# Attention and a feed-forward layer on one core: the second product of the last chunks as Strassen's seven block products

## The chip, the cores and the metric

The program runs on one core of a Trainium2 chip. The metric is the device time of one execution in microseconds (us). The engines are TensorE (PE in the profile; its weight loads are PEld), VectorE (DVE), ScalarE (ACT), GpSimd (POOL) and SyncE (SP, which issues transfers). Each takes its own queue of instructions in order, and an instruction waits at the head of its queue for the semaphores that it names.

## The reference

Sliding-window attention with a linear bias over 8 batches, 8 heads, 576 positions and head width 64; its output, laid out as 4608 tokens of width 512, goes through a feed-forward layer of width 2048. All inputs and outputs are float32.

```python
h = x @ w_in                              # (4608, 512) @ (512, 2048)
g = h * (1.0 / (1.0 + np.exp(-1.702 * h)))
return (g @ w_out).astype(np.float32)     # (4608, 2048) @ (2048, 512)
```

The attention ahead of it is `softmax(q k^T / 8 + slope * -|i - j|)` over the last 128 positions, times `v`.

## The kernel before

Tokens are worked in 18 chunks of 256 (`T`, `NCH`; numbered 0 to 17). The 2048 hidden columns are 16 "f tiles" of 128 (`NF`); two neighbours, 2p and 2p+1, are pair p. A chunk walks over its f tiles in a `Job`. `up` (L947) makes one f tile of the hidden layer with 12 matmuls, each with a moving tile of 256 columns: every float32 operand is split into a high part (a cast to fp32r) and a low part (what the cast left over), and three of the four products of the parts are summed (high by high, high by low, low by high) over four slices of the width 512. ACT then takes the tanh (L961), DVE finishes g (L962), ACT casts it to gh (L497) and POOL takes the rest gl = g - gh (L500). `down` (L969) multiplies this f tile by its rows of w_out: 3 passes (gh by the high part of w, gh by the low part, gl by the high part) for each of the two token halves, 6 matmuls with 512 moving columns, into two banks of PSUM, `acc0` and `acc1`, over all 16 f tiles. `finish` (L982) halves the sums and stores them; for the last chunk DVE and ACT each take half of a row block.

`up` of tile f+1 is put ahead of `down` of tile f in the program, so PE has 12 matmuls to do while ACT, DVE and POOL make g. The attention of later batches is fed in between the f tiles; its last matmuls stand at about 903 us in the trace, and from there on the program holds only the feed-forward layer.

Every operation goes through a planner (`Plan.add`), with a buffer taken from numbered slots of a tag (`buf(pool, shape, dtype, tag, slots)`). Up to a set point (`CUT`) the planner's own order is used; the rest, the last chunks among it, is handed in program order to a scheduler that sets the order in each engine's queue. Which slot an operation's buffer has is fixed before. Tags that matter here: `h` (2 slots of PSUM), `g`, `gh`, `gl` (2 each), `o` (3 slots of 128x512), `xf` (4 slots of 128x1024, the attention's output by chunk), and the PSUM banks `s`, `x`, `t` of the attention. The split weights stay in SBUF as `w1` and `w2`, one tile for each f, with its high and its low part.

## Time and profile before

| | |
|---|---|
| median of 3 runs | 1050.21 us (1050.11 to 1050.41) |
| profiled execution | 1050.36 us, of it the span that the trace covers 1048.6 us |
| PE busy | 1035.2 us, 99% of the span |
| DVE, ACT, POOL busy | 710.6, 620.6, 515.6 us (68%, 59%, 49%) |
| chain that ended last | PE 90%, DVE 6% |

The page of the profile gives the busy time of each engine, the span in 40 slices, the chain of work that ended last, and the costliest groups of instructions. A group's row reads: line, engine, operation, output<-inputs, shapes, count, then busy time and mean ns of one, then the idle time of the engine before them and what ended it. A matmul's recorded length includes its way through the array, so neighbours overlap: the rate is read from how far the starts of a run of matmuls lie apart, which the chain of waits shows.

### The profile page before, as it was taken

The page shows a single profiled execution, that of the slowest core. Times are in us where ns is not written, and L with a number is a line of the kernel's source. Part 1 is how long each engine was busy: PE and PEld are TensorE (multiplying, and loading weights), DVE is VectorE, ACT ScalarE, POOL GpSimd, SP SyncE. Part 2 cuts the span into 40 slices and gives each one's busy share as a digit, 9 for nine tenths or more (in the row PEclk, how much of TensorE's full clock was granted, in tenths as well). Part 3 has the DMA queues.
Part 4 walks back from the last instruction along what each step waited for, and adds up shares of the span by engine and source line. Part 5 has one row for each costly group of instructions (what it writes and reads, how often), then busy time and mean ns, then how long its engine had stood idle before and what let it go on. Part 6 is the DMA issues. An engine that isn't in the chain of part 4 may idle for free.

```text
span 1048.6 us, 21817 instructions
## 1 busy us (share of the span) xinstructions
PE 1035.2 (99%) x6986; PEld 931.0 (89%) x6986; DVE 710.6 (68%) x2418; ACT 620.6 (59%) x1804; POOL 515.6 (49%) x781
## 2 busy tenths in 40 slices
PE   9999999999999999999999999999999999999998
PEld 5777888988988999999999999999999999999997
DVE  8999988898978867444767667666867576412221
ACT  7999877677745665534555556655665566322322
POOL 3344444443423466544655666665766565323232
PEclk9999999999999999999999999999999999999999
DMA  9734233233322222211222223222222120000000
GB/s 342 312 103 132 60 88 100 75 82 104 86 60 68 81 75 69 60 46 29 71 58 60 73 63 89 70 66 59 88 68 85 55 83 17 22 1 22 1 21 21
DMA packets 88033, 80.31 MB, mean 77 GB/s; under 512 B 41776, under 2 KB 78000, under 8 KB 87920
## 3 DMA queue, kind: packets, MB, share of 16 engines
q1 hardware_dynamic: 82736, 69.50, 22.3%
q10 hardware_dynamic: 5184, 9.44, 2.4%
q8 instruction: 55, 0.90, 0.4%
q14 instruction: 58, 0.48, 0.2%
HBM read 69.47 MB, written 9.44 MB: 75 GB/s over the span
## 4 chain that ended last, share of the span: by engine, by line
PE 90%; DVE 6%; issue 2%; ACT 1%; POOL 0%; DVEq 0%; POOLq 0%; ACTq 0%
PE h_ps L953 35%; PE acc L977 35%; PE t_ps L834 5%; PE s_ps L760 5%; PE x_ps L879 5%; PE s_ps L757 1%; PE x_ps L873 1%; DVE pb L779 1%; DVE wc L584 1%; DVE g L962 1%; DVE w_ps L581 1%; PE idle L548 1%; DVE gl L500 1%; DVE xf L924 1%; DVE pl L853 0%
## 5 line engine op out<-in xcount | busy, mean ns | idle before, releaser
L953 PE MATMUL h_ps<-xh,w 128*128 128x256 f32 x2304 | 357.3, 283 | 0.1
L953 PEld LDWEIGHTS h_ps<-xh,w 128*128 128x128 f32 x2304 | 321.2, 188 | 24.3 <-DVE g L962 1.6
L977 PE MATMUL acc<-w,gh 128*128 128x512 f32 x1152 | 320.2, 396 | 0.0
L500 POOL TENSOR_TENSOR gl<-g,gh 128x256 fp32r<-128x256 f32 x225 | 169.1, 752 | 235.6 <-ACT gh L497 178.2
L962 DVE SCALAR_TENSOR_TENSOR g<-g,h_ps 128x256 f32<-128x256 f32 x288 | 120.1, 417 | 186.0 <-ACT g L961 183.7
L961 ACT ACTIVATE g<-h_ps 128x256 f32<-128x256 f32 x288 | 110.2, 383 | 212.9 <-PE h_ps L953 197.4
L977 PEld LDWEIGHTS acc<-w,gh 128*128 128x128 f32 x1152 | 196.0, 188 | 24.4 <-issue 0.2
L953 PE MATMUL h_ps<-xl,w 128*128 128x256 f32 x1152 | 189.4, 279 | 0.0
L977 PE MATMUL acc<-w,gl 128*128 128x512 f32 x576 | 184.3, 397 | 0.0
L953 PEld LDWEIGHTS h_ps<-xl,w 128*128 128x128 f32 x1152 | 160.6, 188 | 4.6
L497 ACT CAST gh<-g 128x256 fp32r<-128x256 f32 x235 | 95.5, 406 | 104.4 <-DVE g L962 97.6
L791 ACT ACTIVATE pb<-pb,mins 128x256 f32<-128x256 f32 (+2 forms) x272 | 132.7, 489 | 39.4 <-DVE mins L779 31.7
L500 POOL TENSOR_TENSOR Q<-rq,Q 64x256 fp32r<-64x256 f32 (+1 forms) x136 | 93.8, 689 | 101.5 <-issue 26.9
L500 POOL TENSOR_TENSOR K<-rk,K 128x384 fp32r<-128x384 f32 (+1 forms) x120 | 108.7, 906 | 61.1 <-PE x_ps L879 19.4
L779 DVE CUSTOM_DVE_ANT_0 pb<-s_ps,bias 128x256 f32<-128x256 f32 (+2 forms) x304 | 111.1, 378 | 10.0 <-PE s_ps L760 4.7
L977 PEld LDWEIGHTS acc<-w,gl 128*128 128x128 f32 x576 | 96.7, 189 | 11.9 <-issue 0.3
L760 PE MATMUL s_ps<-K,Q 128*128 128x256 f32 (+1 forms) x504 | 92.5, 295 | 2.3 <-DVE mins L779 1.3
L834 PE MATMUL t_ps<-ident,pb 128*128 128x128 f32 x516 | 91.4, 273 | 2.7 <-DVE wc L584 2.4
L853 DVE TENSOR_TENSOR pl<-t_ps,ph 128x512 fp32r<-128x512 f32 (+2 forms) x140 | 84.8, 605 | 6.9 <-ACT ph L497 6.3
L497 ACT CAST ph<-t_ps 128x512 fp32r<-128x512 f32 (+2 forms) x134 | 69.6, 519 | 23.9 <-PE t_ps L834 22.7
L760 PEld LDWEIGHTS s_ps<-K,Q 128*128 128x128 f32 x504 | 71.9, 189 | 9.8 <-DVE mins L779 2.0
L813 DVE TENSOR_SCALAR pb<-pb,rec 128x256 f32<-128x256 f32 (+1 forms) x191 | 73.8, 419 | 2.6
(102 smaller groups left out, 1274.3 us busy)
## 6 DMA issues: line engine op xcount, KB each, us to landing
...
```

The source lines that it names most:

```text
L497: (nc.scalar.copy if e == "ACT" else nc.vector.tensor_copy)(dst, src)
L500: (nc.gpsimd if e == "POOL" else nc.vector).tensor_tensor(dst, a, b, ALU.subtract)
L760: nc.tensor.matmul(to, u.Q.t[:, q], ks.t[:, k], start=(z == 0), stop=(z == 1))
L779: add("DVE", lambda b=b, e=e, head=head, ra=ra, rb=rb, cs=cs, on=on: nc.vector.tensor_tensor_reduce(b.p.t[ra:rb, cs:b.end], u.s.t[ra:rb, e ...
L791: nc.scalar.activation(live, live, AF.Exp, bias=u.mins.t[:b.rows, e:e + 1], scale=-1.0, accum_out=u.sums.t[:b.rows, e, 0:1])
L813: (nc.gpsimd if on == "POOL" else nc.vector).tensor_scalar(live, live, rec, None, ALU.mult)
L834: nc.tensor.transpose(u.t.t[:c.n, w:w + b.rows], b.p.t[:b.rows, col:col + c.n], ident[:b.rows, :b.rows])
L853: add("DVE", lambda m=m, a=a, z=z: nc.vector.tensor_tensor(u.pl.t[:m, a:z], u.t.t[:m, a:z], u.ph.t[:m, a:z].bitcast(F32), ALU.subtract), d ...
L953: nc.tensor.matmul(h.t, w.t[:, z, k * P:(k + 1) * P], x[k].t, start=(part == 0 and k == 0), stop=(part == 2 and k == NC - 1))
L961: add("ACT", lambda: nc.scalar.activation(g.t, h.t, AF.Tanh, scale=0.851), act_psum(T), r=[h], w=[g], shift=-NEXT)
L962: add("DVE", lambda: nc.vector.scalar_tensor_tensor(g.t, g.t, 1.0, h.t, ALU.add, ALU.mult), dve_one(T), r=[h], w=[g], shift=-NEXT)
L977: nc.tensor.matmul(acc.t, g.t[:, t * P:(t + 1) * P], w.t[:, z], start=(f == self.f0 and n == 0), stop=(f == self.f1 - 1 and n == 2))
```

## The change

`FAST` names the pairs of f tiles of the last three chunks whose second product is made otherwise: pairs 2 to 6 of chunk 15, and pairs 1 to 6 of chunks 16 and 17; 17 pairs in all. For such a pair the product of a 2x2 block matrix of g (two token halves by two f tiles) and a 2x2 block matrix of w_out (two f tiles by two column halves) is made from seven block products, numbered 1 to 7, in place of eight. Each is again three passes of high and low parts, with 256 moving columns: 21 matmuls in place of 12 with 512 columns.

Three things come beside it. `fold` makes, once for each of pairs 1 to 6, the five sums and differences of blocks of w_out and splits them anew; it is called six times within chunk 15, for pair p+2 at the even tile of pair p, and for pair 1 at f = 10. Its results overwrite parts of `w2` (products 6 and 7) or lie in buffers that the attention no longer needs (`lend`, names `wf_...`). `combine` makes for every fast pair the sums and differences of the blocks of g (`gsum`, `gtrace`) and their parts (`gh`, `gl`, `gd`, `gb`). `gather` adds the products that are held in the banks `s`, `x`, `t` (`m13`, `m45`, `m2`) into the output tile after the last fast pair; products 6 and 7 go straight into `acc0` and `acc1`. Both `wtemp` of `fold` and `gsum`, `gd`, `gb` of `combine` live in the three slots of tag `o`. The bias tables become one tile, so that it can be lent. The store of the last chunk is written by DVE alone.

```diff
+FAST = {NCH - 3: range(2, 7), NCH - 2: range(1, 7), NCH - 1: range(1, 7)}
...
-    bias = [const.tile([P, 2 * P], BF16, name=f"bias{h}") for h in range(H)]
+    bias = const.tile([P, H, 2 * P], BF16, name="bias", tag="bias_0")
...
+    lent = [(att, "ph", 2), (att, "ph", 2), (att, "pl", 2), (att, "pl", 2), (const, "bias", 1), (xp, "xf", XBUFS)]
...
+    def fold(p):
+        f0, f1 = 2 * p, 2 * p + 1
+        half = DM // 2
+        both = buf(xp, [P, 2, DM], F32, "xf", XBUFS, name="wsum")
+        for i, f in enumerate((f0, f1)):
+            on = (nc.vector, "DVE", dve_one(DM)) if i == 0 else (nc.gpsimd, "POOL", pool_two(DM))
+            add(on[1], lambda on=on, i=i, f=f: on[0].tensor_tensor(
+                both.t[:, i], w2[f].t[:, 0].bitcast(F32), w2[f].t[:, 1].bitcast(F32), ALU.add), on[2], r=[w2[f]], w=[(both, i)],
+                port=True, behind=plan.chains["sum"])
+        u, v = (Part(both, i, lambda t, i=i: t[:, i]) for i in range(2))
+        ins = {1: (u, 0, v, 1, ALU.add), 3: (u, 1, v, 1, ALU.subtract), 4: (v, 0, u, 0, ALU.subtract),
...
+        res = {2: Part(w2[f0], "n0", lambda t: t[:, :, :half]), 5: Part(w2[f1], "n1", lambda t: t[:, :, half:])}
...
+        for n, (a, i, b, j, op) in ins.items():
+            at = 0 if temp is None else half
+            if temp is None:
+                held = buf(ffn, [P, DM], F32, "o", 3, name="wtemp")
+            temp = Part(held, at, lambda t, at=at: t[:, at:at + half])
+            if n == 6:
+                m = Part(w2[f0], "n1", lambda t: t[:, :, half:])
+            elif n == 7:
+                m = Part(w2[f1], "n0", lambda t: t[:, :, :half])
+            else:
+                m = lend()
+            (hk, hi), (lk, lo) = side(m, 0), side(m, 1)
+            on, eng, ns = (nc.vector, "DVE", dve_one(half)) if n in (1, 4, 7) else (nc.gpsimd, "POOL", pool_two(half))
+            add(eng, lambda on=on, a=a, i=i, b=b, j=j, op=op, temp=temp: on.tensor_tensor(
+                temp.t, a.t[:, i * half:i * half + half], b.t[:, j * half:j * half + half], op),
+                ns, r=list({id(x): x.key_at() for x in (a, b)}.values()), w=[temp.key_at()], port=True)
+            add("ACT", lambda hi=hi, temp=temp: nc.scalar.copy(hi(), temp.t), act_cast(half), r=[temp.key_at()], w=[hk])
+            on, eng, ns = (nc.vector, "DVE", dve_one(half)) if n in (3, 6) else (nc.gpsimd, "POOL", pool_two(half))
+            add(eng, lambda on=on, hi=hi, lo=lo, temp=temp: on.tensor_tensor(
+                lo(), temp.t, hi().bitcast(F32), ALU.subtract), ns, r=[hk, temp.key_at()], w=[lk], port=True)
+            res[n] = m
...
+        folded[p] = res
...
+            if f // 2 in self.fast:
+                add("ACT", lambda: nc.scalar.activation(g.t, h.t, AF.Tanh, scale=0.851), act_psum(T), r=[h], w=[g], shift=-NEXT)
+                add("DVE", lambda: nc.vector.scalar_tensor_tensor(g.t, g.t, 1.0, h.t, ALU.add, ALU.mult),
+                    dve_one(T), r=[h], w=[g], shift=-NEXT)
+                self.gs[f] = g
+                if f % 2:
+                    self.combine(f // 2)
+                return
...
-                697, r=[g, gh], w=[gl], port=True, shift=-NEXT, ways=less_ways(T), lax=LAX["gl"])
+                697, r=[g, gh], w=[gl], port=True, shift=-NEXT, ways=less_ways(T), lax=LAX["gl"],
+                auto="DVE" if self.fast and f == self.f1 - 1 else "POOL")
...
+        def combine(self, p):
+            a, b = self.gs.pop(2 * p), self.gs.pop(2 * p + 1)
...
+            def cast(x, y, key, to, src, n):
+                add("ACT", lambda: nc.scalar.copy(x.t[:, to], y.t[:, src]), act_cast(n), r=[y], w=[x.key_at(key)], shift=-NEXT)
+            def rest(eng, x, y, h, key, to, src, n):
+                on = nc.vector if eng == "DVE" else nc.gpsimd
+                add(eng, lambda: on.tensor_tensor(x.t[:, to], y.t[:, src], h.t[:, to].bitcast(F32), ALU.subtract),
+                    dve_one(n) if eng == "DVE" else pool_two(n), r=[y, h.key_at(key)], w=[x.key_at(key)], port=True, shift=-NEXT)
...
+            first = [buf(ffn, [P, T], F32R, tag, 2) for tag in ("gh", "gl")]
+            for i, (y, src) in enumerate(((a, lo), (b, hi))):
+                to = slice(i * P, i * P + P)
+                cast(first[0], y, i, to, src, P)
+                rest("POOL", first[1], y, first[0], i, to, src, P)
+            parts(first, (3, 4))
+            both = slice(0, T)
+            sums = buf(ffn, [P, DM], F32, "o", 3, name="gsum")
+            plus("DVE", sums, both, a, both, b, both, ALU.add, T)
+            second = [buf(ffn, [P, T], F32R, tag, 2) for tag in ("gh", "gl")]
+            cast(second[0], sums, 0, both, both, T)
+            rest("DVE", second[1], sums, second[0], 0, both, both, T)
+            parts(second, (5, 2))
+            diffs = slice(T, 3 * P), slice(3 * P, 4 * P)
+            plus("DVE", sums, diffs[0], b, lo, b, hi, ALU.subtract, P)
+            plus("DVE", sums, diffs[1], a, hi, a, lo, ALU.subtract, P)
+            third = buf(ffn, [P, DM], F32R, "o", 3, name="gd")
+            th = [Part(third, z, lambda t, z=z: t[:, z * T:z * T + T]) for z in range(2)]
+            cast(th[0], sums, 0, both, slice(T, DM), T)
+            rest("POOL", th[1], sums, th[0], 0, both, slice(T, DM), T)
+            parts(th, (7, 6))
+            last = buf(ffn, [P, DM], F32R, "o", 3, name="gb")
+            trace = buf(raw, [P, 3 * D], F32, "rv", 2, name="gtrace")
+            corner = [Part(last, z, lambda t, z=z: t[:, z * P:z * P + P]) for z in range(2)]
+            whole = slice(0, P)
+            plus("DVE", trace, whole, a, lo, b, hi, ALU.add, P)
+            cast(corner[0], trace, 0, whole, whole, P)
+            rest("POOL", corner[1], trace, corner[0], 0, whole, whole, P)
+            ms[1] = tuple((x.key_at(), lambda x=x: x.t) for x in corner)
+            self.gs[p] = ms
...
+            if self.apart is None:
+                X = buf(ps, [P, 2, half], F32, "s", 1, name="m13")
+                Y = buf(ps, [P, 2, half], F32, "x", 1, name="m45")
+                Z = buf(ps, [P, 2, half], F32, "t", 2, name="m2")
+                self.apart = {n: (m, i) for n, m, i in ((1, X, 0), (3, X, 1), (4, Y, 0), (5, Y, 1), (2, Z, 0))}
+            ms, ws = self.gs.pop(p), folded[p]
+            for n in (3, 4, 5, 2, 7, 6, 1):
...
+                for k, (g, z) in enumerate(((gh, 0), (gh, 1), (gl, 0))):
+                    wk, w = side(ws[n], z)
+                    def run(n=n, k=k, g=g, w=w, out=out):
+                        nc.tensor.matmul(
+                            out(), g[1](), w(), start=(n in (2, 3, 4) and p == self.fast[0] and k == 0),
+                            stop=(n in (1, 2, 5) and p == self.fast[-1] and k == 2), skip_group_check=True)
+                    add("PE", run, 116, 165, r=[g[0], wk], w=[to if n > 5 else (to, n)], chain="down")
+            if p == self.fast[-1]:
+                self.gather()
...
+                add("DVE", lambda: nc.vector.scalar_tensor_tensor(
+                    o.t[:, t, a:z], src().rearrange("p a n -> p (a n)"), by, o.t[:, t, a:z], ALU.mult, ALU.add), dve_one(z - a),
...
+            halved(0, 0, DM, lambda: X.t, X)
+            halved(1, 0, half, lambda: Y.t[:, :1], Y)
+            halved(1, half, DM, lambda: X.t[:, :1], X)
+            more(0, 0, DM, lambda: Y.t, Y, 0.5)
+            more(0, 0, half, lambda: Y.t[:, 1:], Y, -0.5)
+            more(1, half, DM, lambda: X.t[:, 1:], X, 0.5)
+            more(1, 0, half, lambda: Z.t[:, :1], Z, 0.5)
+            more(1, half, DM, lambda: Z.t[:, :1], Z, -0.5)
...
         def down(self, f):
+            if f // 2 in self.fast:
+                if f % 2:
+                    self.down_fast(f // 2)
+                return
...
+                if self.fast and f == self.f1 - 1:
+                    last.append((n, g, z))
+                else:
+                    add("PE", run, 464, 165, r=[g, (w, z)], w=list(self.acc), chain="down")
+            for t, acc in enumerate(self.acc):
+                for n, g, z in last:
+                    add("PE", lambda t=t, acc=acc, n=n, g=g, z=z: nc.tensor.matmul(
+                        acc.t, g.t[:, t * P:(t + 1) * P], w.t[:, z], start=False, stop=n == 2, skip_group_check=True),
+                        232, 165, r=[g, (w, z)], w=[acc], chain="down")
...
+            if self.fast:
+                o, on = self.out, nc.sync if self.c == NCH - 1 else nc.scalar
                 for t, acc in enumerate(self.acc):
-                    for e, a in (("DVE", 0), ("ACT", half)):
-                        add(e, lambda e=e, t=t, acc=acc, a=a: half_on(e, o.t[:, t, a:a + half], acc.t[:, a:a + half]),
-                            act_psum(half), r=[acc], w=[(o, (t, a))])
+                    add("DVE", lambda t=t, acc=acc: nc.vector.scalar_tensor_tensor(
+                        o.t[:, t], acc.t, 0.5, o.t[:, t], ALU.mult, ALU.add), dve_one(DM), r=[acc], w=[(o, (t,))])
...
+        if j.c in FAST:
+            if j.c == NCH - 3 and f % 2 == 0 and f // 2 + 2 in j.fast:
+                fold(f // 2 + 2)
+            elif j.c == NCH - 3 and f == 10:
+                fold(1)
```

In the rows below a name's number ahead of the last is its slot (`gd_0_14930` lies in slot 0 of its tag). ACT's queue where chunk 14 ends and chunk 15 begins, before (`gh_1_14512` is the cast of f tile 0 of chunk 15):

```order
L961 ACTIVATE g_0_14467<-h_ps_1_14454 128x256
L497 CAST gh_0_14470<-g_0_14467 128x256
L961 ACTIVATE g_1_14509<-h_ps_0_14496 128x256
L497 CAST gh_1_14512<-g_1_14509 128x256
L961 ACTIVATE g_0_14540<-h_ps_1_14527 128x256
L1011 DMA out<-o_0_14522 128x512 x2
L497 CAST gh_0_14543<-g_0_14540 128x256
```

and now (the same cast is `gh_1_14505`):

```order
L658 CAST wf_pl_0_14603<-wtemp_1_14601 128x256
L1045 ACTIVATE g_1_14502<-h_ps_0_14489 128x256
L658 CAST w2_6_0_931<-wtemp_0_14610 128x256
L658 CAST wf_bias_0_14607<-wtemp_0_14610 128x256
L1045 ACTIVATE g_0_14557<-h_ps_1_14544 128x256
L658 CAST w2_7_0_1022<-wtemp_2_14617 128x256
L658 CAST wf_bias_0_14607<-wtemp_1_14601 128x256
L1218 DMA out<-o_0_14515 128x512
L498 CAST gh_1_14505<-g_1_14502 128x256
```

Four casts for `fold`, the tanh of the next f tile and one store stand between the tanh of f tile 0 (`g_1_14502`) and its cast.

POOL's queue late in chunk 15, before (only rests of g and, for the next chunk, of x):

```order
L500 TENSOR_TENSOR gl_0_14859<-g_0_14854,gh_0_14857 128x256
L500 TENSOR_TENSOR gl_1_14885<-g_1_14880,gh_1_14883 128x256
L500 TENSOR_TENSOR xl0_0_14927<-xf_1_12925,xh0_0_14919 128x256
L500 TENSOR_TENSOR xl2_0_14931<-xf_1_12925,xh2_0_14923 128x256
L500 TENSOR_TENSOR gl_0_14911<-g_0_14906,gh_0_14909 128x256
```

and now, from the last rests of pair 4 (`gd_0_14930`, `gb_2_14935`) to those of pair 5, with `fold` of pair 1 between them:

```order
L1070 TENSOR_TENSOR gd_0_14930<-gsum_1_14922,gd_0_14930 128x256
L1070 TENSOR_TENSOR gl_1_15020<-g_0_14951,gh_1_15018 128x128
L1070 TENSOR_TENSOR gl_1_15020<-g_1_15015,gh_1_15018 128x128
L1070 TENSOR_TENSOR gb_2_14935<-gtrace_0_14933,gb_2_14935 128x128
L655 TENSOR_TENSOR wtemp_1_14978<-wsum_2_14975 128x256
L660 TENSOR_TENSOR wf_K2_1_14982<-wtemp_1_14978,wf_K1_0_14980 128x256
L655 TENSOR_TENSOR wtemp_0_14989<-wsum_2_14975 128x256
L660 TENSOR_TENSOR wf_VV_1_14993<-wtemp_0_14989,wf_VV_0_14991 128x256
L660 TENSOR_TENSOR w2_3_0_634<-wtemp_2_14998,w2_3_0_634 128x256
L1070 TENSOR_TENSOR gd_0_15032<-gsum_1_15024,gd_0_15032 128x256
L1070 TENSOR_TENSOR gb_2_15037<-gtrace_1_15035,gb_2_15037 128x128
L1070 TENSOR_TENSOR gl_1_15095<-g_1_15090,gh_1_15093 128x128
```

Five rows for `fold` stand between the rests of two pairs; `wtemp_0_14989` is written in the slot that held `gd_0_14930`.

PE's queue at the same place, before (second product of f tile 11 amid the up product of f tile 13):

```order
L977 MATMUL acc0_0_14547<-w2_11_0_1482,gh_0_14805 128x512
L977 MATMUL acc1_0_14549<-w2_11_0_1482,gh_0_14805 128x512
L977 MATMUL acc0_0_14547<-w2_11_0_1482,gh_0_14805 128x512
L977 MATMUL acc1_0_14549<-w2_11_0_1482,gh_0_14805 128x512
L953 MATMUL h_ps_1_14841<-xh3_0_14486,w1_13_0_1734 128x256
L953 MATMUL h_ps_1_14841<-xh0_0_14480,w1_13_0_1734 128x256
L953 MATMUL h_ps_1_14841<-xh1_0_14482,w1_13_0_1734 128x256
L977 MATMUL acc0_0_14547<-w2_11_0_1482,gl_0_14807 128x512
L977 MATMUL acc1_0_14549<-w2_11_0_1482,gl_0_14807 128x512
L953 MATMUL h_ps_1_14841<-xh2_0_14484,w1_13_0_1734 128x256
```

and now (L1134 is a block product; the last readers of `gd_0_14930`, then what is left until the sums of pair 5, `gh_0_15026`):

```order
L1134 MATMUL acc0_0_14564<-w2_9_0_1265,gd_0_14930 128x256
L1134 MATMUL acc1_0_14566<-w2_8_0_1149,gd_0_14930 128x256
L1029 MATMUL h_ps_1_15077<-xl0_0_14481,w1_13_0_1727 128x256
L1029 MATMUL h_ps_1_15077<-xl1_0_14483,w1_13_0_1727 128x256
L1029 MATMUL h_ps_1_15077<-xl2_0_14485,w1_13_0_1727 128x256
L1029 MATMUL h_ps_1_15077<-xl3_0_14487,w1_13_0_1727 128x256
L1134 MATMUL m45_0_14751<-wf_pb_1_14787,gl_1_15020 128x256
L1134 MATMUL m13_0_14747<-wf_xf_0_14674,gb_2_14935 128x256
L1134 MATMUL m13_0_14747<-wf_Q_0_14781,gh_1_15018 128x256
L1134 MATMUL m13_0_14747<-wf_pb_3_14783,gh_1_15018 128x256
L1134 MATMUL m13_0_14747<-wf_Q_0_14781,gl_1_15020 128x256
L1134 MATMUL m45_0_14751<-w2_11_0_1475,gh_0_15026 128x256 x2
```

Nine matmuls stand between the last reader of `gd_0_14930` and the first reader of `gh_0_15026`. ACT's queue at this place now:

```order
L658 CAST wf_K1_0_14980<-wtemp_1_14978 128x256
L658 CAST wf_K2_0_14985<-wtemp_1_14978 128x256
L658 CAST wf_VV_0_14991<-wtemp_0_14989 128x256
L658 CAST w2_2_0_588<-wtemp_0_14989 128x256
L658 CAST w2_3_0_634<-wtemp_2_14998 128x256
L1066 CAST gh_0_15026<-gsum_1_15024 128x256
L1036 ACTIVATE g_1_15090<-h_ps_1_15077 128x256
```

`gh_0_15026` stands behind the casts of all temporaries of `fold`, two of them made from `wtemp_0_14989`.

## Rows read from the trace of the kernel before

**Rows 1.** The page: busy time by engine; granted clock and POOL in 40 slices.
```profile
PE 1035.2 (99%) x6986; PEld 931.0 (89%) x6986; DVE 710.6 (68%) x2418; ACT 620.6 (59%) x1804; POOL 515.6 (49%) x781
...
POOL 3344444443423466544655666665766565323232
PEclk9999999999999999999999999999999999999999
```
**Rows 2.** Busy time of each engine in four stretches of the end.
```profile
core 0: us, PE busy (x) PEld busy (x) DVE busy (x) ACT busy (x) POOL busy (x), PEclk, DMA share, GB/s
870.00:913.00 43.00, 43.00 (x299) 39.78 (x298) 22.23 (x74) 20.54 (x58) 18.35 (x30) 1.00 0.03 7
913.00:957.00 44.00, 44.00 (x285) 39.90 (x285) 10.40 (x25) 12.48 (x32) 13.74 (x18) 1.00 0.03 13
957.00:1002.00 45.00, 45.00 (x294) 40.92 (x293) 11.81 (x26) 12.98 (x33) 13.30 (x18) 1.00 0.03 12
1002.00:1044.00 42.00, 42.00 (x271) 37.86 (x269) 7.32 (x18) 12.00 (x31) 11.80 (x16) 1.00 0.04 13
```
**Rows 3.** Chain of waits, 912 to 922: start, length, what.
```profile
914.03 1.38 PE h_ps L953 x12
915.42 1.37 PE acc L977 x6
916.79 1.39 PE h_ps L953 x12
```
**Rows 4.** Groups by form, 880 to 1049.
```profile
L500 POOL TENSOR_TENSOR gl<-g,gh 128x256 fp32r<-128x256 f32 x58 | 43.0, 741 | 108.5 <-ACT gh L497 89.6 <-PE acc L977 6.2 <-issue 3.7
...
L962 DVE SCALAR_TENSOR_TENSOR g<-g,h_ps 128x256 f32<-128x256 f32 x57 | 24.0, 421 | 108.9 <-ACT g L961 108.8
L497 ACT CAST gh<-g 128x256 fp32r<-128x256 f32 x58 | 23.6, 408 | 33.2 <-DVE g L962 31.7 <-PE acc L977 1.4
L961 ACT ACTIVATE g<-h_ps 128x256 f32<-128x256 f32 x57 | 21.9, 385 | 75.4 <-PE h_ps L953 74.7 <-POOL xb L900 0.6
...
L500 POOL TENSOR_TENSOR VV<-rv,VV 128x128 fp32r<-128x128 f32 x3 | 1.4, 457 | 0.5 <-ACT VV L497 0.5
...
L497 ACT CAST VV<-rv 128x128 fp32r<-128x128 f32 x3 | 0.9, 300 | 0.3 <-PE x_ps L879 0.3
```
**Rows 5.** Groups by form, whole span: POOL, DVE and ACT on 512 columns.
```profile
L500 POOL TENSOR_TENSOR w<-wc,w 128x512 fp32r<-128x512 f32 x11 | 14.2, 1287 | 12.0 <-ACT g L961 8.2 <-ACT rw L579 2.0 <-ACT w L497 1.6
...
L506 DVE TENSOR_SCALAR o<-acc 128x512 f32<-128x512 f32 x29 | 19.0, 683 | 2.4 <-PE acc L977 2.4
...
L504 ACT ACTIVATE o<-acc 128x512 f32<-128x512 f32 x3 | 1.8, 598 | 0.0
```
**Rows 6.** DVE at L500: shortest, median, longest ns; first and last start.
```profile
L500 DVE TENSOR_TENSOR gl<-g,gh x63: 405/425/1006, 33.0 to 355.5; 128x256 fp32r<-128x256 f32 x63
L500 DVE TENSOR_TENSOR xl<-xf,xh x39: 408/826/1175, 71.8 to 997.8; 128x256 fp32r<-128x256 f32 x39
L500 DVE TENSOR_TENSOR VV<-rv,VV x22: 216/306/628, 177.7 to 352.2; 128x128 fp32r<-128x128 f32 x13, 128x64 fp32r<-128x64 f32 x7, 128x192 fp32r<-128x192 f32 x2
L500 DVE TENSOR_TENSOR w<-wc,w x21: 669/685/1254, 16.0 to 132.8; 128x512 fp32r<-128x512 f32 x21
```
**Rows 7.** Timeline at 951 us, DVE, then POOL: start, length, what.
```profile
951.54 1.84 DVE L500 TENSOR_TENSOR xl<-xf,xh 128x256 fp32r<-128x256 f32 x2
...
951.33 0.89 POOL L500 TENSOR_TENSOR gl<-g,gh 128x256 fp32r<-128x256 f32 x1 [1.82 <-PE h_ps L953]
952.18 1.81 POOL L500 TENSOR_TENSOR xl<-xf,xh 128x256 fp32r<-128x256 f32 x2
```
**Rows 8.** Timeline, one f tile of the last chunk, and a store on ACT's queue.
```profile
1039.45 0.62 PE L953 MATMUL h_ps<-xl,w 128*128 128x256 f32 x4
...
1040.17 0.39 ACT L961 ACTIVATE g<-h_ps 128x256 f32<-128x256 f32 x1 [0.57 <-PE h_ps L953]
1040.59 0.42 DVE L962 SCALAR_TENSOR_TENSOR g<-g,h_ps 128x256 f32<-128x256 f32 x1 [1.43 <-ACT g L961]
...
1041.09 0.41 ACT L497 CAST gh<-g 128x256 fp32r<-128x256 f32 x1 [0.54 <-DVE g L962]
...
1041.59 0.74 POOL L500 TENSOR_TENSOR gl<-g,gh 128x256 fp32r<-128x256 f32 x1 [1.18 <-ACT gh L497]
...
1002.43 0.34 ACTq L1011 DMA_DIRECT2D out<-o  x1
```
**Rows 9.** The end of the chain of waits.
```profile
1040.07 3.90 PE acc L977 x17
1043.97 0.02 issue
1044.00 0.44 DVE o L506
...
1044.45 0.71 ACT o L504 x2
```

More of the change, by code (lines that the diff above doesn't have):

```diff
@@ L590, in decode, with lend @@
         return res
+    lent = [(att, "ph", 2), (att, "ph", 2), (att, "pl", 2), (att, "pl", 2), (const, "bias", 1), (xp, "xf", XBUFS)]
+    for pool, tag, slots, n in (
+            (raw, "rq", 3, 3), (att, "Q", 2, 2), (att, "pb", 5, 5), (raw, "rk", 3, 3), (att, "K1", 2, 2),
+            (att, "K2", 2, 2), (att, "VV", 3, 3)):
+        lent += [(pool, tag, slots)] * n
+    spare = []
+    folded = {}
+    def lend():
+        if not spare:
+            pool, tag, slots = lent.pop(0)
+            if tag in ("bias", "xf"):
+                b = buf(pool, [P, 2, 2, DM // 2], F32R, tag, slots, name=f"wf_{tag}")
+                spare.extend(Part(b, i, lambda t, i=i: t[:, i]) for i in range(2))
+            elif tag in ("ph", "pl"):
+                spare.append(Part(buf(pool, [P, 2, DM // 2], F32R, tag, slots, name=f"wf_{tag}"), 0, lambda t: t))
+            else:
+                pair = []
+                for _ in range(2):
+                    size = 3 * P if tag in ("rk", "K1", "K2", "VV") else 2 * P
+                    pair.append(Part(buf(pool, [P, size], F32R, tag, slots, name=f"wf_{tag}"), 0, lambda t: t[:, :2 * P]))
+                    if len(pair) < 2:
+                        pool, tag, slots = lent.pop(0)
+                spare.append(tuple(pair))
+        return spare.pop(0)
@@ L945, in __init__ @@
             self.gs = {}
+            self.fast = FAST.get(c, ())
+            self.apart = None
         def up(self, f):
@@ L972, in down @@
             gh, gl = self.gs.pop(f)
-            w = w2[f]
+            w, last = w2[f], []
             for n, (g, z) in enumerate(((gh, 0), (gh, 1), (gl, 0))):
```

48 lines of the change are left out of this document (40 added, 8 removed).

## The prediction

> **What bounds the kernel now.** I read the page first, then the busy times of the last 180 us, the chain of waits there, the durations of single operations by form, and last the places where DVE and POOL work side by side. The page says PE: 99% of the span at the full granted clock, 2.4 GHz in the last slices too [rows 1]. In the stretches that the last three chunks fill, PE is busy all the time, while DVE, ACT and POOL have 10 to 14 us of work in 42 to 45 us [rows 2]. So in these chunks only less work on PE can gain, and three engines are two thirds idle. The chain gives PE's true rate: 12 matmuls of 256 columns take 1.38 us and 6 of 512 columns 1.37 us [rows 3], 0.115 and 0.228 us each. An up product has as many weight loads per column as a block product will have, and they already hide at this rate.
>
> **What the change removes.** A pair's second product is now 2 x 1.37 = 2.74 us of PE. The new one is 21 matmuls of 256 columns, 21 x 0.115 = 2.415 us. That is 0.325 us less, for 17 pairs 5.5 us. Nothing else leaves the path, and this is the most that it can give.
>
> **What it adds in chunks 16 and 17.** A fast pair has, on POOL, three rests of 128 columns and one of 256, 3 x 0.457 + 0.741 = 2.1 us; on ACT two tanh, three casts of 128 and two of 256, 2 x 0.385 + 3 x 0.300 (by the casts of the same width) + 2 x 0.408 = 2.5 us [rows 4]; on DVE two g at 0.421, two sums of 256 columns at about 0.41 and three of 128 at about 0.3, 2.6 us [rows 4, 6]. PE needs 2.76 (two up products) + 2.415 = 5.2 us for the pair, so each engine is half idle. Latency: tanh, g, cast and rest follow each other at 0.1, 0.03, 0.08 and 0.09 us [rows 8]. From the end of the odd tile's up product, the sums of g are cast after 0.10 + 0.39 + 0.03 + 0.42 + 0.03 + 0.41 + 0.04 + 0.41 = 1.8 us, and the last rest on POOL is done after some 3.5 us. In the new order PE has the next tile's up product, product 3 and in most pairs a second up product ahead of the others, 1.38 + 0.345 + 1.38 = 3.1 us, and product 1 stands 1.7 us behind that. Nothing waits; I take 0 here. If that cover went, a wait of 0.3 us in each of 11 pairs would cost 3.3 us.
>
> **The end.** Before, the last store could be issued 1045.16 - 1043.97 = 1.19 us after the last matmul [rows 9]. Now products 1 are complete 12 matmuls of 512 columns, 2.74 us, before the end. ACT takes 0.60 us for the first halving; DVE then has one addition of 512 columns and three of 256, and the two final ones of 512: 3 x 0.683 + 3 x 0.421 = 3.31 us [rows 4, 5]. That ends 0.1 + 0.60 + 3.31 - 2.74 = 1.27 us after the last matmul: 0.1 us later than before.
>
> **What it adds in chunk 15.** Here `fold` comes on top. One fold is on POOL one sum of 512 columns and five operations of 256: 1.287 + 5 x 0.741 = 5.0 us; on DVE as many of its own kinds, 0.685 + 5 x 0.41 = 2.7 us; on ACT five casts, 2.0 us [rows 4 to 6]. With `combine` POOL has 7.1 us for a pair where PE has 5.2. The folds begin when the attention ends, so POOL starts with a lead and loses it. Three places decide.
>
> First, f tile 0 of the chunk. Its tanh can end 0.10 + 0.39 us after its up product. ACT then takes, in order, four casts for `fold`, a tanh, a store (0.34) and only then this tile's cast: 4 x 0.408 + 0.385 + 0.34 + 0.408 = 2.77 us, 3.3 us in all [rows 4, 8]. PE has 14 matmuls of 256 columns and 2 of 512 in between, 2.07 us. It waits 1.2 us.
>
> Second, POOL from the last rest of pair 2 to the last of pair 5, where the folds of pairs 5 and 6 and of pair 1 lie: 18 operations of 256 columns, 9 of 128 and 2 of 512, 18 x 0.741 + 9 x 0.457 + 2 x 1.287 = 20.0 us. PE has 163 matmuls of 256 columns in that stretch, 18.7 us. POOL's lead at its start is what pair 2 leaves: its last rest can be done 3.5 us after the up product of f tile 5, and PE wants it after 6.1 us (53 matmuls), so 2.6 us. Alone, POOL would be in time by 1.3 us.
>
> But DVE has 21 operations of 256 columns, 2 of 512 and 9 of 128 with both inputs in SBUF in the same stretch, and such operations get in POOL's way. At 951.5 us two of them and three of POOL's overlap: the two on DVE take 0.92 us each where 0.41 is the least, and POOL's two take 1.81 us where 2 x 0.741 would be 1.48 [rows 4, 6, 7]; a typical one of chunk starts takes 0.826 [rows 6]. So a DVE operation of 256 columns costs POOL 0.9 - 0.741 = 0.17 us. By width, 21 x 0.17 + 2 x 0.34 + 9 x 0.09 = 5.1 us if POOL is always busy. Then POOL is late by 5.1 - 1.3 = 3.8 us.
>
> Third, the slots of `o`. The second half of `wtemp_0_14989` is written by POOL where `gd_0_14930` lay, thus after PE has read that. Then ACT casts it, casts another, and casts the sums of pair 5: 0.741 + 3 x 0.408 + about 0.2 of handovers = 2.2 us, in which PE has 9 matmuls, 1.0 us. PE waits 1.2 us here whatever else happens, and through that wait POOL's other work does not start earlier.
>
> Bounds for the second and third together: 1.2 us (only the slot) from below. From above DVE's own queue, if each of its operations with two SBUF inputs is held up as in rows 7: 21 x 0.92 + 2 x 1.25 (the longest of 512 columns) + 9 x 0.6 (the longest of the narrow ones) + 6 g x 0.421 = 29.7 us against PE's 18.7, 11.0 us late [rows 4, 6, 7]. I take POOL's 3.8 and the slot's 1.2, 5.0 us: POOL is busy nearly all the time in this stretch, which is the case of rows 7, but DVE is not, and meets a free port in part.
>
> The early part of the folds (the sums for pair 2) lies amid the attention of chunk 14, where POOL has 18 us of work in 43 [rows 2]; I cost it at nothing, and its 1.3 us at most if POOL's cover there is gone. The merged bias tables move no work; 0.
>
> **Sum.** -5.5 + 0.1 + 1.2 + 5.0 = +0.8 us against the profiled execution's own 1050.36 us (span 1048.6 and 1.8 around it), 1051.2; that execution lies 0.15 us above the median of the runs, so 1051.0 us as a median.
>
> **The rivals.** A measurement of this kernel tells about 0.2%, 2.1 us, from no change.
>
> (A) My forecast: waits of chunk 15 between 3.3 and 7.5 us eat the gain. 1048.1 to 1052.3 us, likeliest 1051.0. For it stand POOL's sum and the slots. Chance 0.40.
>
> (B) Only the two fixed waits are real, 1.2 + 1.2 us: POOL and DVE meet seldom, as on those copies of rows 6 that took the least time. -5.5 + 0.1 + 2.4 = -3.0, 1047.2 us. For it: three engines have room outside of this chunk, and POOL's sum alone fits. Against it: in chunk 15 both engines work on the same tiles back to back. Chance 0.28.
>
> (C) DVE becomes the bound in pairs 3 to 5, since each of its operations with two SBUF inputs waits for the POOL operation that runs: 11.0 + 1.2 us of waits, +6.8, 1057.0 us at the full price. It decides for slower as soon as waits pass 7.5 us, thus DVE's queue 18.7 + 6.3 = 25.0 us there; between 15.1 us (all at their least: 21 x 0.41 + 2 x 0.685 + 9 x 0.3 + 2.5) and 29.7 that is two thirds of the way, a mean of 0.75 us for 256 columns. Rows 6 and 7 have 0.826 and 0.92, which speaks for it; that DVE also runs while POOL waits for ACT's casts speaks against it. Chance 0.32; I expect 1053 to 1056 us in this case.
>
> The Trainium skill, page "SBUF — State Buffer", section "Who interferes with whom", states a lock where I sum a cadence: a DVE operation with two SBUF inputs and a GpSimd operation exclude each other for the whole instruction. By it each DVE operation would add its own length to POOL's queue, an estimate of 12.6 us in the three pairs where I have 5.1, and the change would end at about +8 us, on the side of (C). The trace agrees in kind, not in size: the pair takes 0.92 us there, not 0.41 + 0.741 = 1.15 [rows 4, 6, 7], so the sum stays with 0.92.
>
> That the change would not shorten PE's work (a matmul of 256 columns costing more than half of one of 512) is excluded by rows 3.
>
> **How the numbers follow.** Faster by over 0.2% is case B, 0.28; within 0.2% case A, 0.40; slower case C, 0.32. The range reaches from the price of B, 1047.3 us, to where C's own range ends with less than a tenth above, 1055.5 us. Within A alone it is 1048.1 to 1052.3.
>
> **What would show it.** In the new profile PE's work must be 5.5 us less, and PE must have idle time in chunk 15 alone: about 1 us ahead of the first down product of f tile 0, waiting for ACT, and most of the rest in pairs 3 to 5, ahead of products 5 and 2 and of the rests of 6 and 7. Chunks 16 and 17 must each be shorter by 6 x 0.325 = 2.0 us and show no wait. DVE's sums of 256 columns in chunk 15 must have a mean between 0.6 and 0.9 us, and near 0.41 would be case B. The forecast is wrong if PE waits in chunks 16 and 17, if the tail grows by more than 0.5 us, or if the attention of chunk 14 gets longer.

## The result, and the profile after

The changed kernel takes 1063.35 us (1062.24 to 1064.47, four runs) where the kernel before took 1050.24 us (1050.11 to 1050.41): a ratio of 1.0125, 95% interval 1.0107 to 1.0142. It is slower by 13 us. Case C of the prediction came, at about twice its full price of 6.8 us. The profiled execution is one of 1062.38 us, its span 1060.6 us.

The page after, busy time by engine and four of its lines of 40 slices; it answers to [rows 1]:

```profile
PE 1036.1 (98%) x7139; PEld 937.4 (88%) x7139; DVE 779.5 (73%) x2557; ACT 644.2 (61%) x1892; POOL 558.6 (53%) x848
...
PE   9999999999999999999999999999999999889998
...
DVE  8999988899978868445758576757766685876464
...
POOL 3353544344423566445656566656766574884342
PEclk9999999999999999999999999999999999999999
```

Apart from the last slice, PE is below 9 only where chunk 14 ends and chunk 15 runs, and there DVE and POOL go up to 8. DVE's busy time grew by 68.9 us over the whole span; the operations that were added come to some 55 us at the lengths that they have alone (17 x 1.8 for the sums of g, 6 x 2.7 for the folds, 3 x 2.8 for the gathering and a last rest).

Busy time in stretches of the last 200 us, from the last 50 us of the attention to the last matmul; it answers to [rows 2]:

```profile
core 0: us, PE busy (x) PEld busy (x) DVE busy (x) ACT busy (x) POOL busy (x), PEclk, DMA share, GB/s
855.00:880.00 25.00, 24.14 (x167) 21.91 (x166) 21.07 (x71) 14.98 (x46) 18.01 (x27) 1.00 0.19 55
...
904.00:920.00 16.00, 12.60 (x77) 10.46 (x75) 12.11 (x21) 6.29 (x18) 13.32 (x16) 1.00 0.00 1
920.00:973.00 53.00, 46.14 (x331) 43.40 (x332) 41.30 (x80) 23.60 (x69) 38.39 (x51) 0.97 0.03 11
973.00:1015.00 42.00, 42.00 (x339) 41.12 (x339) 24.17 (x62) 18.36 (x54) 17.08 (x29) 1.00 0.04 14
1015.00:1056.00 41.00, 41.00 (x325) 39.76 (x324) 20.68 (x53) 17.31 (x52) 15.24 (x27) 1.00 0.04 14
```

Chunks 16 and 17 (the last two rows) show no wait of PE, as forecast; they are 1.6 and 1.9 us shorter than before, where 2.0 us each were forecast. Between 904 and 973 us DVE is busy for 53 of 69 us; in a chunk of before it was 10 of 44.

What PE waited for from 860 us on, but for two waits of 0.5 us or less (line, releaser, sum, times, longest):

```profile
PE m L1134 <- DVE gl L1070: 3.0, 2, 2.6
PE h_ps L1029 <- DVE g L1046: 2.8, 2, 2.4
PE m L1134 <- ACT gh L1066: 2.3, 2, 2.0
PE h_ps L1029 <- DVE g L1037: 1.5, 2, 1.4
PE h_ps L1029 <- DVE xh L498: 0.6, 2, 0.3
```

The releasers are DVE, and ACT's cast of a sum that DVE had just made. POOL, which the forecast held to be the late engine, is not in the list. It does stand in the chain of waits behind it: from 917 to 962 us the chain has 20.0 us of DVE and 7.2 us of POOL, all of POOL's before 933.4 us. DVE's queue ahead of the longest wait (timeline, with POOL's operations at the time; PE's row at its end):

```profile
945.39 0.92 POOL L655 TENSOR_TENSOR wtemp<-wsum 128x256 f32<-128x256 f32 x1
...
945.63 0.95 DVE L655 TENSOR_TENSOR wtemp<-wsum 128x256 f32<-128x256 f32 x1
...
947.18 2.12 DVE L1075 TENSOR_TENSOR gsum<-g 128x128 f32<-128x128 f32 x2
...
947.81 1.34 POOL L634 TENSOR_TENSOR wsum<-w 128x512 f32<-128x512 f32 x1
949.12 0.77 POOL L660 TENSOR_TENSOR w<-wtemp,w 128x256 fp32r<-128x256 f32 x1
949.23 1.21 DVE L634 TENSOR_TENSOR wsum<-w 128x512 f32<-128x512 f32 x1
...
950.36 0.41 DVE L1070 TENSOR_TENSOR gl<-gsum,gh 128x256 fp32r<-128x256 f32 x1
...
950.82 0.51 PE L1134 MATMUL m<-w,gl 128*128 128x256 f32 x2 [2.60 <-DVE gl L1070]
```

Two sums of 128 columns take 0.82 and 1.38 us (one row, 2.12 us), and `wsum` of a later fold stands ahead of the `gl` that PE needs. As soon as POOL is done (949.89 us) DVE's operations take 0.41 us again.

The same groups of DVE over 855 to 973 us, mean ns of one after the comma; they answer to [rows 5, 6]:

```profile
L655 DVE TENSOR_TENSOR wtemp<-wsum 128x256 f32<-128x256 f32 x18 | 13.4, 768 | 6.3 <-PE acc L1134 3.7 <-POOL wsum L634 2.0 <-POOL gd L1070 0.6
L1046 DVE SCALAR_TENSOR_TENSOR g<-g,h_ps 128x256 f32<-128x256 f32 x24 | 9.9, 414 | 6.3 <-ACT g L1045 6.2
L634 DVE TENSOR_TENSOR wsum<-w 128x512 f32<-128x512 f32 x6 | 5.6, 940 | 0.1
...
L1075 DVE TENSOR_TENSOR gsum<-g 128x128 f32<-128x128 f32 x10 | 5.4, 562 | 0.1
```

Where the time went is read from five landmarks in the timelines, all of them PE's: the start of the last matmul of the attention, and the start of the last second-product matmul of chunks 14, 15, 16 and 17. Each is set against the kernel before, so that a column's steps are what each stretch lost. (`no_fold` and `fold_only` are told of below.) The profiled executions of `no_dve_fold`, `after_pin` and `early_fold` lost 3.9 us in their first 24 us, so only distances within these traces are used.

| us against before | attention's end | chunk 14 | chunk 15 | chunk 16 | last matmul |
|---|---|---|---|---|---|
| before, at | 902.6 | 913.6 | 957.2 | 1001.5 | 1043.8 |
| changed | +1.7 | +3.6 | +15.6 | +14.0 | +12.1 |
| no_fold | -0.1 | -0.1 | -1.1 | -2.8 | -4.8 |
| fold_only | +1.5 | +3.4 | +10.6 | +9.9 | +9.9 |

### The profile page after: what moved, and what is told of

It reads as the page before. It is cut to its first block, busy times and chain, and to the rows that moved or that the text cites. A ratio compares the mean times of both kernels' runs of the same rounds, so it can differ in the third digit from the quotient of the medians.

```text
span 1060.6 us, 22523 instructions
## 1 busy us (share of the span) xinstructions
PE 1036.1 (98%) x7139; PEld 937.4 (88%) x7139; DVE 779.5 (73%) x2557; ACT 644.2 (61%) x1892; POOL 558.6 (53%) x848
## 4 chain that ended last, share of the span: by engine, by line
PE 82%; DVE 11%; issue 3%; ACT 2%; POOL 1%; DVEq 0%; ACTq 0%; POOLq 0%
PE h_ps L1029 32%; PE acc L1177 28%; PE s_ps L834 5%; PE t_ps L908 5%; PE x_ps L953 5%; PE m L1134 2%; PE x_ps L947 1%; PE s_ps L831 1%; PE acc L1134 1%; DVE g L1046 1%; DVE pb L853 1%; DVE xf L998 1%; DVE wc L585 1%; DVE pl L927 1%; DVE w_ps L582 1%
## 5 line engine op out<-in xcount | busy, mean ns | idle before, releaser
L1177 PE MATMUL acc<-w,gh 128*128 128x512 f32 x1004 | 279.9, 397 | 0.3 <-DVE o L507 0.3
L501 POOL TENSOR_TENSOR gl<-g,gh 128x256 fp32r<-128x256 f32 x188 | 141.5, 753 | 147.6 <-ACT gh L498 104.4
L1177 PEld LDWEIGHTS acc<-w,gh 128*128 128x128 f32 x1004 | 170.9, 189 | 22.1 <-issue 0.6
L1045 ACT ACTIVATE g<-h_ps 128x256 f32<-128x256 f32 x254 | 97.0, 382 | 150.9 <-PE h_ps L1029 134.6
L1046 DVE SCALAR_TENSOR_TENSOR g<-g,h_ps 128x256 f32<-128x256 f32 x254 | 105.6, 416 | 82.5 <-ACT g L1045 80.3
L1177 PE MATMUL acc<-w,gl 128*128 128x512 f32 x502 | 161.0, 398 | 0.0
L498 ACT CAST gh<-g 128x256 fp32r<-128x256 f32 x201 | 81.4, 405 | 86.4 <-DVE g L1046 80.3
L1177 PEld LDWEIGHTS acc<-w,gl 128*128 128x128 f32 x502 | 84.3, 189 | 10.2 <-issue 0.3
L834 PEld LDWEIGHTS s_ps<-K,Q 128*128 128x128 f32 x504 | 71.8, 189 | 10.6 <-DVE mins L853 2.8
```

Of the source, the lines that this page charges most:

```text
L498: (nc.scalar.copy if e == "ACT" else nc.vector.tensor_copy)(dst, src)
L501: (nc.gpsimd if e == "POOL" else nc.vector).tensor_tensor(dst, a, b, ALU.subtract)
L834: nc.tensor.matmul(to, u.Q.t[:, q], ks.t[:, k], start=(z == 0), stop=(z == 1))
L1045: add("ACT", lambda: nc.scalar.activation(g.t, h.t, AF.Tanh, scale=0.851), act_psum(T), r=[h], w=[g], shift=-NEXT)
L1046: add("DVE", lambda: nc.vector.scalar_tensor_tensor(g.t, g.t, 1.0, h.t, ALU.add, ALU.mult), dve_one(T), r=[h], w=[g], shift=-NEXT)
L1177: nc.tensor.matmul(acc.t, g.t[:, t * P:(t + 1) * P], w.t[:, z], start=(f == self.f0 and n == 0), stop=(f == self.f1 - 1 and n == 2), skip_ ...
```

## The experiments

Theory D: the meeting of DVE and POOL on operations with both inputs in SBUF makes each of DVE's take twice its time; DVE's queue, with g and the sums of g in it behind fold's operations, is what PE waits for. Rivals: P, POOL's queue (the forecast); S, the mere number of fold's instructions ahead of g; K, `combine` rather than `fold`. Times are medians against a kernel before of 1050.1 to 1050.2 us.

**no_fold**: the products without the folds.

```diff
-                fold(f // 2 + 2)
+            for p in range(1, 7):
+                folded[p] = {n: Part(w2[2 * p + n % 2], ...) for n in range(1, 8)}
```

> The sums of w_out's blocks are left out (each block product reads an unsummed block of w_out), the products and the sums of g stay. Theory D (DVE's queue: fold's operations with two SBUF inputs wait there for POOL's, and g and the sums of g stand behind them): nothing of fold is left, so no wait is left; 1050.2 - 5.5 + 0.1 = 1044.8 us, between 1044.3 and 1046. Rival K (the sums of g, made by combine, are what PE waits for): waits in chunk 15 stay, above 1049 us.

Measured 1045.73 us, ratio 0.9956 (0.9938 to 0.9973), and not one wait of PE after 855 us. K falls. It also measures the first term of the sum: 4.8 us by the landmarks, 0.28 us a pair, where 5.5 was forecast. The last matmul starts 4.8 us before the span's end in the kernel before and 4.7 us before it here and in the changed kernel, so the end costs nothing.

**fold_only**: the folds without the products.

```diff
-            self.fast = FAST.get(c, ())
+            self.fast = ()
```

> The folds stay where they are, every second product is made as before (from w_out's tiles, parts of which the folds overwrite), the end of the last chunk as before. Theory D: the losses ahead of chunk 15 and at its start (about 6 us) stay whole, and a good part of the 8 us of pairs 2 to 6; 1056 to 1064 us. Rival K: fold alone costs nothing, 1050 to 1052 us.

Measured 1059.98 us, ratio 1.0091 (1.0061 to 1.0122). The loss up to chunk 14's end is nearly the changed kernel's (3.4 of 3.6 us), and 7.2 us more come in chunk 15. Folds alone cost 9.9 us, and 16.9 us together with `combine` (changed less no_fold in the table). One of PE's waits after 855 us is for POOL here:

```profile
PE acc L1177 <- POOL gl L501: 2.0, 2, 1.1
```

From 917 to 968 us the chain of waits has 19.0 us of POOL and 2.8 us of DVE. So without `combine` it is POOL's queue that is late, as rival P has it; with `combine` on DVE it is mostly DVE's.

**no_pool_fold** and **no_dve_fold**: one engine's half of the folds left out.

```diff
+            if eng == "POOL":   # in the other kernel "DVE"
+                temp = ...      # a block of wsum that the other engine made; no instruction
+            else:
                 add(eng, ...)
```

> POOL's part of fold is left out (its sums and rests; what needed them reads DVE's), DVE's and ACT's part stays: DVE issues the same instructions. Theory D: DVE's sums of 256 columns go from a mean of 0.77 to between 0.41 and 0.5 us, PE's waits after 855 us from about 14 to below 3 us, 1045 to 1048 us. Rival S (the number of fold's instructions in DVE's queue, contention or not): waits of 8 us or more stay, above 1053 us. Theory P (as forecast: POOL's queue is what is late): 1045 to 1048 us too, but what is left of waits is for ACT or POOL.

> DVE's part of fold is left out, POOL's (5.0 us for each pair) and ACT's stay. Theory D: DVE holds only what combine and the g need, PE waits below 3 us, 1045 to 1048 us. Rival S the same. Theory P: POOL's own queue of 20.0 us against PE's 18.7 with a lead of 2.6 us fits only just, and combine's sums of g still meet it; waits for POOL's rests of 1 to 4 us in pairs 3 to 5, 1046 to 1049 us.

Measured 1047.07 us (ratio 0.9965, 0.9951 to 0.9980) and 1049.62 us (0.9983, 0.9965 to 1.0002). What PE waits for in `no_pool_fold` after 855 us, and DVE's sums there (L669 is L655 of the changed kernel):

```profile
PE h_ps L1046 <- DVE g L1063: 1.1, 1, 1.1
```

```profile
L669 DVE TENSOR_TENSOR wtemp<-wsum 128x256 f32<-128x256 f32 x18 | 8.4, 484 | 0.8 <-PE acc L1151 0.4 <-POOL gd L1087 0.2 <-PE m L1151 0.2
```

The same 18 sums now take 0.48 us, not 0.77, and 1.1 us of waits is left. S falls here: the number of instructions did not change. Over no_fold, DVE's half costs 1.3 us by itself, POOL's 3.9 us, and both together 17.6 us: 12 us come only when both halves run. This counts everything that one half does to the other, the results that DVE awaits from POOL too. Of these the changed kernel shows 2.6 us ahead of DVE's `wtemp` (2.0 and 0.6 in the first group of DVE above). Longer operations weigh more: from 855 to 973 us DVE's 67 operations with both inputs in SBUF take 18.4 us more than at the lengths that they have with no operation of POOL beside them (0.41 us for 256 columns, 0.29 for 128; 0.68 for 512, from the kernel before).

`no_dve_fold` missed D's range by 1.6 us and P's by 0.6, and chunk 15 is 3.3 us longer there than in no_fold. POOL's queue is not what is late: PE's waits after 855 us, 1.5 us in all, end with DVE or with ACT's cast of a sum, and no POOL operation stands in the chain of waits from 917 to 965 us. DVE's sums of 128 columns stand in it, 0.73 us each in the mean where POOL's half of the folds runs beside them. This is D's mechanism on `combine`'s own operations, which D's number left out.

**all_dve**: the same folds, all on DVE.

```diff
-            on = (nc.vector, "DVE", dve_one(DM)) if i == 0 else (nc.gpsimd, "POOL", pool_two(DM))
+            on = (nc.vector, "DVE", dve_one(DM))
```

and so for the sums and the rests of a fold.

> All of fold's sums and rests are made by DVE, none by POOL; the same work otherwise. Theory D (the price lies in the meeting of the two engines: an operation of DVE with two SBUF inputs takes 0.41 us alone, 0.77 and more beside POOL): a fold is 10 x 0.41 + 2 x 0.685 = 5.5 us on DVE, six are 33 us; with some 20 us of older work and 9 us of combine DVE has 62 us where PE has 55, so it is still the bound, but less than before: 1047 to 1054 us. Rival S (the number of fold's instructions ahead of g in DVE's queue decides): DVE has twice as many of them, waits double, above 1068 us.

Measured 1054.19 us, ratio 1.0039 (1.0024 to 1.0054), the last matmul of the profiled execution 9.1 us earlier than in the changed kernel. DVE has twice the sums, and they are short:

```profile
L655 DVE TENSOR_TENSOR wtemp<-wsum 128x256 f32<-128x256 f32 x30 | 13.2, 484 | 0.9 <-POOL gd L1070 0.6 <-PE acc L1134 0.2
```

The same work on one engine in place of two saves 9 us, which speaks for D most plainly; S, which had over 1068 us for twice the instructions, falls. The median lies 0.2 us over D's range. But 8.5 us over no_fold stay: from 914 to 964 us the chain of waits has 18.4 us of DVE and none of POOL (one wait of PE, 1.0 us, is for a rest of POOL's). So about half of the folds' price goes when the two engines no longer meet over them, and half stays, mostly as DVE's load.

**late_fold**: block products in chunks 16 and 17 alone, the fold of a pair two tiles after its use in chunk 15.

```diff
-FAST = {NCH - 3: range(2, 7), NCH - 2: range(1, 7), NCH - 1: range(1, 7)}
+FAST = {NCH - 2: range(1, 7), NCH - 1: range(1, 7)}
-            if j.c == NCH - 3 and f % 2 == 0 and f // 2 + 2 in j.fast:
+        if j.c == NCH - 3 and f % 2 == 0 and f >= 4:
+            fold(f // 2 - 1)
```

> Only chunks 16 and 17 are made with block products; in chunk 15 the fold of pair p stands two f tiles after the pair's own use, and chunk 15 is otherwise as before. PE's work shrinks by 12 x 0.27 to 0.33 = 3.2 to 3.9 us. Theory D: with no fold while the attention ends and with no combine in chunk 15, the meeting of DVE and POOL costs DVE 6 x (5 x 0.9 + 1) = 33 us in a chunk of 44 us where its older work is 10 us, just below PE; waits of 0 to 4 us: 1046.5 to 1051 us. If each fold costs PE what it does in fold_only (9.9 us for six) whatever its place: 1056 to 1057 us.

Measured 1058.74 us, ratio 1.0079 (1.0062 to 1.0096): above both ranges. The attention ended 1.9 us later than before and chunk 14 2.8 us later, though no fold stands there in the program. The scheduler sends the first sums of folds far ahead of their place, DVE's first `wsum` at 858.1 us (in the changed kernel 857.9), so the place in the program decides little.

**after_pin**: the changed kernel with each sum of a fold held in its queue behind the g of its own f tile (on POOL behind the rest of g).

```diff
+            if op.hold:
+                tc.add_manual_dep(op.made, op.hold.made.name, ...NoSync...)
```

> The changed kernel with its folds at their places, but each sum of a fold (on DVE and on POOL) is held in its queue behind the g, or the rest of g, of the f tile at which the program has it: nothing of a fold can start amid the attention any more. Theory D (DVE and POOL together have more work in chunk 15 than PE): the loss ahead of chunk 15 (1.7 us in the attention, about 4 at its end) goes, but the folds come later and pairs 2 to 6 wait longer, 8 to 14 us; 1056 to 1064 us in all. Theory S (only the order was wrong): the waits go with the order, 1046 to 1050 us.

Measured 1069.82 us, ratio 1.0163 (1.0122 to 1.0203), above both ranges. The attention runs free (chunk 14 takes 55.4 us from the last chunk's end, before 55.4), and chunk 15 takes 64.6 us, before 43.6. Busy time, and PE's largest wait after 855 us:

```profile
905.00:920.00 15.00, 15.00 (x101) 13.78 (x101) 7.76 (x17) 4.41 (x12) 7.06 (x10) 1.00 0.05 20
920.00:970.00 50.00, 36.61 (x234) 33.30 (x233) 40.57 (x69) 22.37 (x66) 45.03 (x54) 0.89 0.02 6
```

```profile
PE m L1138 <- ACT gh L1068: 10.1, 4, 3.7
```

With all folds packed into chunk 15 POOL is busy for 45 of 50 us and DVE for 41: in this order there is no room for them. Holding the sums behind g does not bring the time back, so that only the order was wrong falls as a theory. The chain of waits from 918 to 983 us has 16.9 us of POOL and 8.9 us of DVE, so here POOL's queue is the later one. D's number missed the clock too, which stood at 0.89 of full speed over these 50 us; this cost at most 5.5 us, since PE also waited in part of that time.

**early_fold**: the same folds in chunks 8 to 13, kept in DRAM and loaded where fold stood.

```diff
+            d = scratch[p, n] = buf(dram, [P, 2, half], F32, ...)
+            add("SP", lambda: nc.sync.dma_start(d.t, m.t.bitcast(F32)), ...)
...
+        if 1 <= j.c - EARLY <= 6:
+            if f == 1:
+                sums(j.c - EARLY)
+            elif f in (2, 4, 7, 10, 13):
+                fold_early(j.c - EARLY, {2: 1, 4: 3, 7: 4, 10: 6, 13: 7}[f])
```

> The folds are made in chunks 8 to 13, one block sum at every second or third f tile, written to DRAM, and loaded from there at the places where fold stood; 17 pairs as in the changed kernel. Theory D: in chunks 8 to 13 DVE and POOL have 30 to 40% of their time left and PE has other work at every wait, so the folds are hidden there; what is left is no_fold's time: 1045.5 to 1047 us. Rival: the folds cost PE as much wherever they are: 1055 us and more; or the loads (7.9 MB in some 45 us, 175 GB/s, against 233 GB/s over the first 100 us of the trace) come late: waits on DMA in chunk 15.

Measured 1050.52 us, ratio 1.0005 (0.9993 to 1.0017). From the attention's end to the last matmul it takes 137.0 us, no_fold 136.5: the loads are hidden. The median's other 4.3 us were lost earlier: PE idled at four ends of chunks (near 536, 592, 647 to 652 and 760 to 766 us), 3.4 us of it in all. POOL's timeline at one of them, and DVE's row:

```profile
642.78 0.46 POOL L503 TENSOR_TENSOR VV<-rv,VV 128x128 fp32r<-128x128 f32 x1
644.88 1.82 POOL L638 TENSOR_TENSOR wsum<-w 128x512 f32<-128x512 f32 x1 [1.64 <-DMA out<-o]
...
644.84 0.69 DVE L638 TENSOR_TENSOR wsum<-w 128x512 f32<-128x512 f32 x1 [0.97 <-DMA out<-o]
```

`wsum` lies in the buffer of the chunk's output and waits at the head of both queues until the store has landed; g and its rest stand behind it. Neither theory had this.

**early_pin** and **early_pin_dve**: early_fold with the sums held behind the g of their f tile, the first one two f tiles later; in the second kernel all of the early folds are on DVE.

```diff
-            if f == 1:
+            if f == 3:
...
+            op.hold = holds[on[1]]
```

> As early_fold, but each sum of a fold is held in its engine's queue behind the g (DVE) or the rest of g (POOL) of its own f tile, and the first sum of a pair comes two f tiles later, so that no sum waits at the head of a queue for the store of a chunk's output to land (in early_fold DVE idled 0.97 us and POOL 1.64 us there, and PE lost 4.6 us at four chunk boundaries). Theory D: the losses at the boundaries fall to 0 to 1.5 us: 1045.5 to 1047.5 us, clearly below both kernels. Rival: the folds' mere work in the middle costs PE: 1049 to 1051 us as in early_fold.

> As early_pin, with all of the early folds on DVE and none on POOL. Theory D: nothing waits for POOL's rests of g any more, DVE has 5.5 us more in each of six chunks of 54 us where it is 70% busy: 1045.5 to 1047 us, no more than early_pin. Rival (POOL is the one with room there, DVE the tighter engine): 0.5 to 3 us above early_pin.

Measured 1045.14 us (ratio 0.9952, 0.9940 to 0.9964) and 1045.40 us (0.9962, 0.9949 to 0.9976), no different from each other. Both beat both kernels, and 1045.1 us is no_fold's time (1045.7) or better: the folds are free there. PE waits for nothing after 400 us, and in the last chunks it is busy throughout (`early_pin`; compare [rows 2]):

```profile
913.00:957.00 44.00, 44.00 (x343) 42.49 (x343) 23.58 (x58) 17.17 (x51) 16.89 (x28) 1.00 0.09 27
957.00:1002.00 45.00, 45.00 (x357) 43.75 (x356) 24.81 (x63) 19.05 (x56) 17.89 (x31) 1.00 0.06 22
```

## Why the prediction was wrong

What held: PE's work shrinks and nothing else leaves the path; chunks 16 and 17 show no wait; the end of the last chunk costs nothing; fold in chunk 15 is what eats the gain; and at least half of the price, 9 to 12 of 17.6 us, is one of DVE and POOL meeting.

The first term was mis-sized: 4.8 us in place of 5.5. The rate of 0.115 us was read from up products that run alone; where they alternate with block products, runs of the chain come out at 0.115 to 0.119 us a matmul, and 21 of them at 0.1185 would be 2.49 us, a saving of 0.25 a pair. That the alternation causes it was not tried. The sum for the end missed one addition: there are four of 256 columns, not three, 0.4 us more. This changed nothing, since DVE still waited 0.2 us for PE's last sums.

The step that failed is the choice of the engine that pays. "So a DVE operation of 256 columns costs POOL 0.9 - 0.741 = 0.17 us": the pair's 0.9 us was right (three sums of DVE took 2.69 us beside POOL at 916 us), but DVE pays most of it, 0.9 - 0.41 = 0.5 us, and DVE's queue also carries g. From 855 to 973 us POOL's 91 operations of 128, 256 or 512 columns took 6.9 us more than alone, DVE's 67 took 18.4 us more. I had DVE's sum by this price, 29.7 us against PE's 18.7, kept it as a bound and took POOL's 3.8 us, since "POOL is busy nearly all the time in this stretch, which is the case of rows 7, but DVE is not". DVE was busy for 41 of 53 us in chunk 15.

The price by width failed too: "9 x 0.09" for the narrow operations. A sum of 128 columns took 0.56 us in the mean and 1.38 at the longest, since it is held until POOL's operation ends, however narrow it is. The trace shows it: from 855 to 973 us 43 operations of DVE with both inputs in SBUF began with more than 0.2 us of a POOL operation still to run, and each ended 0.15 us (128 columns), 0.28 us (256) or 0.55 us (512) after POOL's did. In the timeline above, the sums of 128 columns end at 949.30 us and POOL's `wsum` at 949.15; DVE's `wsum` ends at 950.44 and POOL's rest at 949.89. POOL's operations that begin amid one of DVE's end 0.59 us (256 columns) after it. Each of these figures is 0.13 to 0.15 us less than the operation takes alone.

"The early part of the folds ... lies amid the attention of chunk 14 ...; I cost it at nothing, and its 1.3 us at most": it cost 1.8 us by the attention's end and 1.9 more by chunk 14's last matmul (changed less no_fold). I went by POOL's load there, 18 us of 43 [rows 2]. DVE is the tighter engine, 22 of 43, and it makes the next chunk's xh, whose casts stood behind `wsum`; two of PE's waits are for them.

"It waits 1.2 us" at f tile 0 of chunk 15, for ACT's queue: PE waited 2.4 us there, for the bank of h that DVE's g had yet to read, behind three sums and a halving.

```profile
916.39 2.69 DVE L655 TENSOR_TENSOR wtemp<-wsum 128x256 f32<-128x256 f32 x3 [1.95 <-POOL wsum L634]
919.00 0.68 DVE L507 TENSOR_SCALAR o<-acc 128x512 f32<-128x512 f32 x1
919.60 0.40 DVE L1046 SCALAR_TENSOR_TENSOR g<-g,h_ps 128x256 f32<-128x256 f32 x1
```

ACT's cast of this g itself waited 0.27 us for DVE. The slot of `o` (1.2 us) is part of what is left: the 2.0 us before 959.91 us end with ACT's cast of pair 5's sums, and DVE's `wtemp` had waited 3.7 us for PE's last reader of that slot (first group of DVE above). How much of the 2.0 us is the slot was not taken apart.

A term was missing: the clock. After the wait of 2.6 us PE ran at half speed for 3.4 us, which costs 1.7 us (last section).

In sum, chunk 15 lost 13.0 us by the folds (16.7 less 3.7 by the table's columns, changed less no_fold) where 6.2 were forecast: waits of 9.2 us, 1.7 us of clock, and 2.1 us that the list of waits does not show (a matmul's recorded 0.28 us reach 0.16 us past the start of the next one at full rate, so a gap is longer than listed). Case C, with 12.2 us of waits at its full price, had the engine and nearly the size for chunk 15; what it lacked is the early part, the clock and the smaller saving.

The Trainium skill, page "SBUF — State Buffer", section "Who interferes with whom", states an exclusive lock between a DVE instruction with two SBUF inputs and a GpSimd instruction that reads SBUF. What the prediction made of it, +8 us, was the better side and the better size. I set it aside because a pair of equal operations took 0.92 and not 1.15 us. That cadence came again (0.90), but it does not speak against the lock: the 0.28 and 0.59 us by which the operations of 256 columns end after each other make 0.87 us, so the two do exclude each other but for some 0.14 us of each recorded length.
